# Transposed sums through ScalarE and GpSimd, and the second quad's stacks three rounds later, in a sliding-window attention kernel

## The chip, the cores and the metric

The kernel runs on one core of a Trainium2 chip. The metric is the device time of one launch in microseconds; the time of a kernel is the median of several runs. A profile is one further execution, recorded by the hardware profiler; its time in the trace is the span.

## What is computed

Four residual layers over a sequence of 2048 tokens with 576 features: attention, spectral filter, attention, spectral filter. The weights are the same both times.

```python
S, D, H, Dh, W = 2048, 576, 32, 18, 256

def A(x, wqkv, wo):                      # sliding-window attention
    q, k, v = split_heads(x @ wqkv)      # 32 heads of 18
    s = q @ k.T * Dh ** -0.5
    s = where((i - j >= 0) & (i - j < W), s, -1e9)
    return merge_heads(softmax(s) @ v) @ wo

def B(x, w_r, w_i):                      # global filter
    return irfft2(rfft2(x) * (w_r + 1j * w_i))

for _ in range(2):
    x = x + A(layernorm(x), wqkv, wo)
    x = x + B(layernorm(x), w_r, w_i)
```

All is in float32. The output is x.

## The kernel before

**Stages.** The program is straight-line code made by Python loops, one stage for each layer: attention, filter, attention, filter. The change lies in the attention stages alone (`layer_a`, called for layer 0 and again for layer 1). In the profiled execution the bursts described below begin at about 132 us in layer 0 and at about 884 us in layer 1; the mixed part, with projections among the attention work, ends at about 420 and 1175 us, and the output projection follows.

**Precision.** Operands of the projections and scores are split in a high and a low part, so that several products are summed to one result. A projection of 128 rows for 512 tokens (`proj`) is 14 matmuls of 128x128 by 128x512 into one PSUM buffer; each of these matmuls is one *projection step* (line L798). When the 14 are done, ScalarE copies the high part to `sg` (L810), Vector makes the low part (L813), and a DMA puts both into `qk_d` in device memory (L815). Eight projections come ahead of everything else; 28 more, 392 steps, are in the list `pj` and are dealt out among the attention work, 70 of them in `opening`, 322 in `bursts`.

**Quads, blocks and rounds.** The 32 heads are eight quads of four. A quad has 16 blocks of 128 tokens. A *round* x is one block of one quad: x = 16 n + i for block i of quad n, 128 rounds in all. The four heads of a round lie as two pairs in two halves of the partitions.

- `score_max` (L855, L857): a matmul gives the scores of a block against the window's three blocks in a PSUM buffer of tag "S"; Vector adds the mask and keeps the maximum of each row.
- `m_rows(n, c)` (L868 to L875): the maxima of four blocks are transposed, ScalarE makes `mt` of them, and four small DMAs put them as extra rows into the stack of q, so that the next matmul subtracts them.
- `exps` (L892, L893, L895, L898): the scores are computed again transposed, with the maximum subtracted, into a buffer of tag "E"; ScalarE takes the exponent; once a round GpSimd sets what lies outside the window to zero by two masks over all four heads.
- `part` (L912, L917): products of the exponents with the values, with a column of ones behind the values, are summed in the bank `U`: 18 sums and the denominator for each head and token. Every fourth block ScalarE copies the bank to `us`.
- `norm(n, c)` (L926 to L936): four transposes turn `us` so that tokens lie on partitions, into a PSUM buffer that `turned` picks; Vector takes the reciprocal of the denominators (L929) and multiplies the sums by it (L931) straight from PSUM; a DMA (L936) puts the result into `o_d`.

The buffer of `turned` is of tag "E" in the opening, of tag "S" (the three buffers that the scores use in turn) while projections are left, and of tag "pj" afterwards. There are 31 norms in a layer; the last group of blocks of the last quad is done by other code at the stage's end, which the change leaves as it is.

**Stacks.** The scores read q and k from the stacks `qs` and `ks`, two of each, used by even and odd quads. `stack_load(n, c)` fills 512 tokens of one quad's stacks from `qk_d` by twelve DMAs of 72 KB each (L830), all on the SP queue. SP takes its instructions in program order; the rows of `m_rows` (for n > 0 or c > 1), the outputs of `norm`, the `qk_d` writes and the loads of values and weights are on the same queue. `loads(t)` says at which round a stack is called: for the second quad at rounds t = 0, 4, 8 and 12, for later quads at t = 16 n - 20 + 4 c.

**Order.** The scores run `LEAD` = 10 rounds ahead of the exponents: round x of the exponents stands beside round x + 10 of the scores. The second quad's scores begin at round 6. `bursts` writes the order out by hand. Burst k holds three score matmuls and three exponent matmuls, since a round has four of each. Three bursts in every eight or so then hold products with the values (`values`); the others hold projection steps. The steps are cut into 23 units, each 14 steps over the bursts up to `ends[i]`, dealt out as evenly as it goes (`steps`), two to five in a burst. A burst with projection steps may also take a task from `due`, maxima rows first and then norms: two projection steps are written ahead of the task, the rest behind it.

**Names in the profile.** `tpo` is the transposed tile of a norm, `rc` the reciprocal, `o` its result, `tpm` the transposed maxima, `qs<-qk_d` and `ks<-qk_d` a stack's loads, `qs<-mt` the rows of maxima, `ofree<-o_d` the load of the attention's result for the output projection.

The call of the stacks before:

```python
c, r = divmod(t + (16 if n == 1 else 20) - NT * n, 4)
if r == 0 and 0 <= c < 4:
    stack_load(n, c)
```

Of the kernel before, what the change touches and what calls it, by code (L numbers as in the profile page):

```python
# [8 lines left out]
F32 = mybir.dt.float32  # L9
# [9 lines left out]
NT = 16  # L19
# [589 lines left out]
def layer_a(tc, ident, eps, bp, src, dst, wqk_d, wv_d, wo_d, dc_d, gc_d, dram, copy, wvs, second, spectral, share):  # L609

    nc = tc.nc
    V, A, T, P = nc.vector, nc.scalar, nc.tensor, nc.gpsimd
# [14 lines left out]
    if True:  # L627
# [134 lines left out]
        with ExitStack() as c2:  # L762
            wp = c2.enter_context(tc.tile_pool(name="a2", bufs=2))
# [8 lines left out]
            for j in range(2):  # L772
                q = wp.tile([128, 2, S], F32R, name=f"qs{j}", bufs=1)
                k = wp.tile([128, 2, S], F32R, name=f"ks{j}", bufs=1)
# [85 lines left out]
            def turned(name):  # L860

                tag = "E" if done < 70 else "S" if done < len(pj) else "pj"
                return pp.tile([128, 4, 128], F32, tag=tag, name=name, bufs=1 if tag == "pj" else 3)
# [59 lines left out]
            def norm(n, c):  # L923
                tp = turned(f"tpo{n}_{c}")
                for a in range(4):
                    T.transpose(tp[:, a], us[n, c][:, a * 128:a * 128 + 128], ident)  # L926
                tv = tp.rearrange("p a (h e) -> p (a h) e", e=32)
                rc = wp.tile([128, 16, 1], F32, tag="rc", name=f"rc{n}_{c}", bufs=2)
                V.reciprocal(rc, tv[:, :, 18:19])  # L929
                o = wp.tile([128, 4, 72], F32, tag="o", name=f"o{n}_{c}", bufs=2)  # L930
                V.tensor_mul(o.rearrange("p a (h e) -> p (a h) e", e=18), tv[:, :, 0:18], rc.to_broadcast([128, 16, 18]))  # L931
                lo, hi = 72 * n, 72 * n + 72
                for a, f0, f1 in ((o_d, 0, 448), (o7_d, 448, 576)):
                    b, e = max(lo, f0), min(hi, f1)
                    if b < e:
                        nc.sync.dma_start(a[c * 512:(c + 1) * 512, b - f0:e - f0].rearrange("(a p) e -> p a e", a=4), o[:, :, b - lo:e - lo])  # L936
# [13 lines left out]
            pj = [f for i in range(2, 9) for c in range(4) for f in proj(i, c, c % 2 if i == 2 else c == 0 and i == 3)]  # L950
# [4 lines left out]
            def loads(t):  # L955
                if t + LEAD in (0, 2):
                    stack_load(0, 2 + (t + LEAD) // 2)
                for n in range(1, NQ):
                    c, r = divmod(t + (16 if n == 1 else 20) - NT * n, 4)
                    if r == 0 and 0 <= c < 4:  # L960
                        stack_load(n, c)
                if t + LEAD == 5:
                    v_load(0)
                if t + 12 in range(NT, NX, NT):
                    v_load((t + 12) // NT)
# [27 lines left out]
            def bursts():  # L993

                es = [(x, pair, hp) for x in range(MIX) for pair in range(2) for hp in range(2)]
                ss = [(x + LEAD, pair, 1 - hp) for x, pair, hp in es]
                parts = [(x, half) for x in range(MIX - 2) for half in range(2) if x % NT]
                values = {(4 * x + 7) // 3 + 2 for x in range(0, MIX - 2, 2)}
                ends = [3] + [max(k - 1 for k in values if k - 1 <= 4 + 134 * (i + 1) // 22) for i in range(22)]
                steps = {}  # L1000
                for i, end in enumerate(ends):
                    ks = [k for k in range(ends[i - 1] + 1 if i else 0, end + 1) if k not in values]
                    steps.update({k: 14 // len(ks) + (z < 14 % len(ks)) for z, k in enumerate(ks)})
                at = 70
                for k in range(-(-len(es) // 3)):
                    e, c = es[3 * k:3 * k + 3], ss[3 * k:3 * k + 3]
                    for x, pair, hp in e:
                        if pair == hp == 0:
                            loads(x)
                            assert not any(source(p) == x - 6 for p in parts)  # L1010
                    score_max(*c[0])
                    for f in e:
                        exps(*f)
                    for f in c[:0:-1]:
                        score_max(*f)
                    remainders()

                    new, took = [], 0
                    spread = at == len(pj)
                    while parts and (took < 430 or source(parts[0]) < e[0][0] - 3 if spread else took == 0 or parts[0][0] % 2 or parts[0][1]):  # L1020
                        if (4 * source(parts[0] if spread else (parts[0][0] | 1, 1)) + 3) // 3 + 2 > k:
                            break
                        x, half = parts[0]
                        if took and half == 0 and (x % 4 == 0 or x % NT == 1):
                            break
                        parts.pop(0)
                        part(x, half)
                        took += lasting((x, half))
                        if half and x % 4 == 3:
                            new.append((norm, *divmod(x // 4, 4)))  # L1030

                    due.sort(key=lambda z: z[0] is norm)
                    tasks = [] if took and not spread else due[:1 + (len(due) > 2)]
                    del due[:len(tasks)]
                    n = steps.get(k, 0)
                    for f in pj[at:at + min(2, n)]:
                        yield f
                    for f, *a in tasks:
                        f(*a)
                    for f in pj[at + 2:at + n]:  # L1040
                        yield f
                    at += n

                    full = (3 * k + len(e)) // 4 + LEAD - 1
                    if (3 * k) // 4 + LEAD - 1 < full and full % 4 == 3:
                        new.append((m_rows, *divmod(full // 4, 4)))
                    due.extend(new)
                    for x, pair, hp in e:
                        if pair == hp == 1:
                            behind(x)  # L1050
                remainders()
                assert at == len(pj)
                for p in parts:
                    part(*p)
                    if p[1] and p[0] % 4 == 3:
                        due.append((norm, *divmod(p[0] // 4, 4)))
# [59 lines left out]
            for k in range(4):  # L1116
                tp = pp.tile([128, 512], F32, tag="E" if k else "pj", name=f"tpz{k}", bufs=3 if k else 1)[0:32]
                for a in range(4):
                    T.transpose(tp[:, 128 * a:128 * a + 128], us[NQ - 1, 3][:, 4 * k + a:512:16], ident)
                tv = tp.rearrange("p (a h e) -> p a h e", a=4, h=4)  # L1120
                rc = wp.tile([128, 4, 4, 1], F32, tag="rc", name=f"rcz{k}", bufs=2)[0:32]
# [5 lines left out]
            tp = pp.tile([128, 512], F32, tag="pj", name="tpl", bufs=1)  # L1127
# [58 lines left out]
```

## Time and profile before

| | us |
|---|---|
| median of 3 runs | 1508.76 |
| lowest and highest | 1503.93, 1511.95 |
| profiled execution, device time | 1516.93 |
| its span in the trace | 1515.2 |

The profiled execution is 8.17 us above the median of the other three, and 1.73 us of its time lie outside its span. Its mean granted TensorE clock is 0.989 of full speed. In rows of the profile PE is TensorE's matmul, PEld its weight load, DVE is Vector, ACT is ScalarE, POOL is GpSimd, SP (SPq) the queue that issues most DMAs. A row of the timeline gives start and duration in us, engine, line, operation, tiles and shapes, how many alike, and in brackets the idle time before and what ended it by the profile. A row of groups gives the count, then busy us and the mean in ns, then idle time before. A row of windows gives the stretch and its length, then busy time and count of each engine, the granted clock, the DMA engines' busy share and GB/s.

### The profile page before, as it was taken

The numbers are of one execution on the slowest core, as the hardware profiler recorded it, in microseconds if no ns is written. First come the engines' busy times: TensorE is split into PE (matmuls) and PEld (weight loads), VectorE is DVE, ScalarE is ACT, GpSimd is POOL, SyncE is SP. The second block draws the span as 40 slices with busy tenths as digits, with TensorE's granted clock in tenths as the row PEclk, the third lists the DMA queues.
The fourth block names the chain that finished last, engine by engine and source line by source line (L and its number), as shares of the span: only waits on it lengthen the run. The fifth ranks groups of instructions, "written<-read, shape, count | busy, mean of one in ns | idle before, by whom it ended". The sixth has DMA issues, their size and how long they took to land.

```text
span 1515.2 us, 34681 instructions
## 1 busy us (share of the span) xinstructions
PE 1447.9 (96%) x12124; PEld 1105.0 (73%) x12124; DVE 968.8 (64%) x3152; ACT 790.0 (52%) x1900; POOL 623.0 (41%) x1026
## 2 busy tenths in 40 slices
PE   7999999999999899999999999999999998999998
PEld 7975566666656799759999756666666568997598
DVE  5328787878883555447852377878788835554476
ACT  5524667666675443224454246667666754442243
POOL 2173345445454333243421833444444543322434
PEclk9999999999999999999999999999999999999999
DMA  6755556655545365767663556565554454657664
GB/s 194 199 168 182 182 179 195 181 177 168 157 134 160 120 217 184 240 204 236 240 168 92 179 185 176 170 166 152 153 153 131 129 160 137 212 187 237 211 209 141
DMA packets 203132, 267.64 MB, mean 177 GB/s; under 512 B 103183, under 2 KB 108303, under 8 KB 201999
## 3 DMA queue, kind: packets, MB, share of 16 engines
q1 hardware_dynamic: 194510, 245.41, 53.4%
q10 hardware_dynamic: 7808, 15.62, 3.1%
q0 software_dynamic: 640, 4.39, 1.0%
q8 instruction: 97, 1.59, 0.5%
q14 instruction: 77, 0.62, 0.1%
HBM read 166.71 MB, written 102.00 MB: 177 GB/s over the span
## 4 chain that ended last, share of the span: by engine, by line
PE 70%; DMA 10%; DVE 6%; ACT 4%; POOL 2%; issue 2%; SPq 1%; ACTq 0%; POOLq 0%; DVEq 0%
PE pj L798 15%; PE S L855 11%; PE U L912 10%; PE ops L555 6%; PE E L892 5%; PE vps L738 4%; PE pf L202 3%; PE pz L215 3%; DMA qs<-mt 3%; DMA ofree<-yd 2%; PE pq L313 2%; PE p L294 2%; PE pi L361 2%; PE tpo L926 2%; PE po L382 2%
## 5 line engine op out<-in xcount | busy, mean ns | idle before, releaser
L857 DVE CUSTOM_DVE_ANT_0 jk<-S,mask 128x384 bf16<-128x384 f32 (+2 forms) x1024 | 491.5, 529 | 129.2 <-PE E L892 71.4
L893 ACT ACTIVATE P<-E 128x384 f32<-128x384 f32 (+2 forms) x1024 | 409.5, 476 | 172.2 <-PE E L892 137.2
L895 POOL TENSOR_SCALAR_AFFINE_SELECT P<-P 128x512 f32<-128x512 f32 x256 | 162.4, 634 | 370.2 <-ACT P L893 347.9
L855 PE MATMUL S<-ks,qs 63*128 63x384 f32 (+2 forms) x1024 | 281.6, 373 | 4.2 <-DMA qk_d<-sg 2.4
L892 PE MATMUL E<-qs,ks 64*128 64x384 f32 (+2 forms) x1024 | 223.7, 373 | 7.9 <-DMA qs<-mt 4.5
L855 PEld LDWEIGHTS S<-ks,qs 63*128 63x128 f32 x1024 | 145.1, 185 | 114.7 <-DVE m L857 69.0
L912 PE MATMUL U<-P,vq 128*19 128x128 f32 (+1 forms) x3840 | 188.4, 329 | 1.0 <-ACT us L917 1.0
L798 PE MATMUL pj<-xh,wqh 128*128 128x512 f32 x360 | 156.9, 436 | 2.8 <-ACT vt L742 1.7
L912 PEld LDWEIGHTS U<-P,vq 128*19 128x19 f32 x3840 | 96.0, 98 | 78.9 <-issue 21.2
L898 POOL TENSOR_SCALAR_AFFINE_SELECT P<-P 128x512 f32<-128x512 f32 x224 | 142.0, 634 | 0.0
L892 PEld LDWEIGHTS E<-qs,ks 64*128 64x128 f32 x1024 | 112.8, 185 | 23.9 <-ACT P L893 14.2
L555 PE MATMUL ops<-oroom 128*128 128x288 f32 x840 | 123.8, 304 | 4.4 <-DVE oroom L538 3.0
L798 PE MATMUL pj<-xh,wql 128*128 128x512 f32 x360 | 125.8, 421 | 0.4 <-POOL wql L460 0.4
L798 PE MATMUL pj<-xl,wqh 128*128 128x512 f32 x288 | 120.7, 419 | 0.0
L555 PEld LDWEIGHTS ops<-oroom 128*128 128x128 f32 x840 | 115.9, 193 | 6.2 <-DVE oroom L538 4.0
L798 PEld LDWEIGHTS pj<-xh,wqh 128*128 128x128 f32 x360 | 67.7, 188 | 34.7 <-issue 11.3
L171 POOL TENSOR_TENSOR eo<-xn 128x287 f32<-128x287 f32 x32 | 26.1, 816 | 153.4 <-ACT xn L169 142.3
L813 DVE TENSOR_TENSOR sg<-pj,sg 128x512 fp32r<-128x512 f32 x72 | 49.5, 687 | 58.2 <-ACT sg L810 58.1
L857 DVE DVE_READ_ACCUMULATOR2_ANT m<- 128x1 f32 x1024 | 84.9, 83 | 0.0
L361 PE MATMUL pi<-oroom 128*128 128x256 f32 (+1 forms) x576 | 77.6, 289 | 5.8 <-ACT oroom L346 5.1
L798 PEld LDWEIGHTS pj<-xh,wql 128*128 128x128 f32 x360 | 64.6, 190 | 23.0 <-issue 11.2
L361 PEld LDWEIGHTS pi<-oroom 128*128 128x128 f32 (+1 forms) x576 | 73.1, 187 | 7.6 <-ACT oroom L346 5.8
(177 smaller groups left out, 2575.2 us busy)
## 6 DMA issues: line engine op xcount, KB each, us to landing
qk_d<-sg SPq DMA_DIRECT2D x56, 512.0 KB
qs<-qk_d SPq DMA_DIRECT2D x384, 72.0 KB
ks<-qk_d SPq DMA_DIRECT2D x384, 72.0 KB
v_d<-vt SPq DMA_DIRECT2D x32, 304.0 KB
vq<-v_d SPq DMA_DIRECT2D x16, 608.0 KB
yd<-ye SPq DMA_DIRECT2D x32, 290.0 KB
wt<-in_w SPq DMA_DIRECT2D x16, 580.0 KB
x<-ofree SPq DMA_DIRECT2D x32, 288.0 KB
```

Source lines behind the costliest of these rows:

```text
L361: T.matmul(o, z[:, sl, c, lo:lo + m], mo, start=k == 0, stop=k == 5)
L555: self.nc.tensor.matmul(self.ps[u][n][:, 0:288], x, self.w[p][:, wk * D + n * 288:wk * D + n * 288 + 288], start=first and i == 0, stop=la ...
L738: T.matmul(ps[:, n, 0:288], xT(xk, c), w[:, wk, n * 288:(n + 1) * 288], start=i == 0, stop=i == len(ks) - 1)
L798: T.matmul(box["ps"].rearrange("r (n p) -> r n p", n=NT) if second else box["ps"], w[:, wk], x, start=s == 0, stop=s == len(ks) - 1)
L813: V.tensor_sub(rest[:, 1], by, rest[:, 0].bitcast(F32))
L855: T.matmul(ps[:, 0:N], q[b:b + 63, pair, i * 128:i * 128 + 128], k[b:b + 63, pair, lo:hi], start=True, stop=True)
L857: V.tensor_tensor_reduce(out=jk[:, 0:N], in0=ps[:, 0:N], in1=mask[:, 384 - N:384], scale=1.0, scalar=-3e38, op0=ALU.add, op1=ALU.max, accu ...
L892: T.matmul(ps[:, 0:nq], k[b:b + 64, pair, j * 128:j * 128 + 128], q[b:b + 64, pair, j * 128:j * 128 + nq], start=True, stop=True)
L893: A.activation(p[:, hl_, 0:nq], ps[:, 0:nq], AF.Exp, scale=SC)
L895: P.affine_select(out=p[:, :, 0:128], in_=p[:, :, 0:128], pattern=[[0, 4], [1, 128]], compare_op=ALU.is_ge, fill=0.0, base=0, channel_mult ...
L898: P.affine_select(out=p[:, :, 256:384], in_=p[:, :, 256:384], pattern=[[0, 4], [-1, 128]], compare_op=ALU.is_gt, fill=0.0, base=0, channel ...
L912: T.matmul(U[32 * h:32 * h + 19, (q0 % 4) * 128:(q0 % 4) * 128 + 128 * (q1 - q0)], vts[n][:, j, h], pt[n, j][:, h, (q0 - j) * 128:(q1 - j) ...
```

## The change

In `norm` the four transposes are followed by a ScalarE copy of 19 of each 32 columns from PSUM into a new tile `ts` in SBUF (one buffer). The reciprocal reads `ts` instead of PSUM and stays on Vector. The multiply reads `ts` and runs on GpSimd (`P`) instead of Vector. The last group's code at the stage's end still uses Vector.

In `loads` the second quad's stacks are called at t = 3, 7, 11 and 15, three rounds later each. Their first calls thereby move from bursts 0, 5, 10 and 16 to bursts 4, 9, 14 and 20. The calls for other quads stay. Stack (2,0) is called at t = 12, which was the round of stack (1,3) and is now ahead of it.

In `bursts` the units and their ends stay, but the steps of a burst are worked out as it is written: what is left of the unit over the bursts left in it, rounded up, and one more (at most five, and leaving two for each burst that follows) where the burst holds a norm and is not its unit's last. Later bursts of the unit get fewer. The total is the same. In bursts with fewer than four steps one step, not two, is written ahead of the task.

```diff
@@ norm
-                tv = tp.rearrange("p a (h e) -> p (a h) e", e=32)
+                ts = wp.tile([128, 16, 19], F32, tag="ts", name=f"ts{n}_{c}", bufs=1)
+                A.copy(ts, tp.rearrange("p a (h e) -> p (a h) e", e=32)[:, :, 0:19])
                 rc = wp.tile([128, 16, 1], F32, tag="rc", name=f"rc{n}_{c}", bufs=2)
-                V.reciprocal(rc, tv[:, :, 18:19])
+                V.reciprocal(rc, ts[:, :, 18:19])
                 o = wp.tile([128, 4, 72], F32, tag="o", name=f"o{n}_{c}", bufs=2)
-                V.tensor_mul(o.rearrange("p a (h e) -> p (a h) e", e=18), tv[:, :, 0:18], rc.to_broadcast([128, 16, 18]))
+                P.tensor_mul(o.rearrange("p a (h e) -> p (a h) e", e=18), ts[:, :, 0:18], rc.to_broadcast([128, 16, 18]))
@@ loads
-                    c, r = divmod(t + (16 if n == 1 else 20) - NT * n, 4)
+                    c, r = divmod(t + (13 if n == 1 else 20) - NT * n, 4)
@@ bursts
-                steps = {}
-                for i, end in enumerate(ends):
-                    ks = [k for k in range(ends[i - 1] + 1 if i else 0, end + 1) if k not in values]
-                    steps.update({k: 14 // len(ks) + (z < 14 % len(ks)) for z, k in enumerate(ks)})
+                unit = {k: i for i, end in enumerate(ends) for k in range(ends[i - 1] + 1 if i else 0, end + 1)}
...
-                    n = steps.get(k, 0)
-                    for f in pj[at:at + min(2, n)]:
+                    n = 0
+                    if k in unit and k not in values:
+                        gaps = sum(z not in values for z in range(k, ends[unit[k]] + 1))
+                        rest = 70 + 14 * (unit[k] + 1) - at
+                        n = -(-rest // gaps)
+                        if gaps > 1 and any(f is norm for f, *a in tasks):
+                            n = min(5, n + 1, rest - 2 * (gaps - 1))
+                    early = 1 if n < 4 else 2
+                    for f in pj[at:at + min(early, n)]:
                         yield f
                     for f, *a in tasks:
                         f(*a)
-                    for f in pj[at + 2:at + n]:
+                    for f in pj[at + early:at + n]:
                         yield f
```

## The prediction

> **What bounds the kernel now.** I read the page first: the span, the busy shares and the split of the chain that ended last.
>
> ```profile
> span 1515.2 us, 34681 instructions
> PE 1447.9 (96%) x12124; PEld 1105.0 (73%) x12124; DVE 968.8 (64%) x3152; ACT 790.0 (52%) x1900; POOL 623.0 (41%) x1026
> PE 70%; DMA 10%; DVE 6%; ACT 4%; POOL 2%; issue 2%; SPq 1%; ACTq 0%; POOLq 0%; DVEq 0%
> ```
>
> TensorE is busy for 96% of the span and is 70% of the chain, so an edit that leaves its work alone gains only where TensorE waits, and loses only where it makes TensorE wait. Next come the windows (busy time and count of PE, PEld, DVE, ACT, POOL, then clock, DMA share, GB/s) of layer 0's attention: all engines from 189.38 to 420, then the score matmuls L855 alone.
>
> ```profile
> 189.38:420.00 230.62, 229.92 (x2289) 143.96 (x2288) 185.75 (x732) 158.55 (x400) 110.45 (x178) 1.00 0.59 175
> 189.38:420.00 230.62, 93.14 (x337) 48.05 (x337) 1.00 0.59 175
> ```
>
> 337 score matmuls at three to a burst are 112 bursts, 230.62 / 112 = 2.06 us each. Vector is busy for 81% of this stretch, GpSimd for 48%, ScalarE for 69%. "PE busy" counts a matmul that is waiting in the pipeline too, so the stalls have to be read from the weight loads. Here are the loads of two neighbouring bursts; the first holds a norm (norm is the step that the change rewrites), the second feels it.
>
> ```profile
> 258.07 0.18 PEld L855 LDWEIGHTS S<-ks,qs 63*128 63x128 f32 x1 [0.21 <-DVE m L857]
> 258.36 0.19 PEld L855 LDWEIGHTS S<-ks,qs 63*128 63x128 f32 x2
> 258.80 0.19 PEld L798 LDWEIGHTS pj<-xh,wqh 128*128 128x128 f32 x1 [0.26 <-DVE sg L813]
> ...
> 260.14 0.18 PEld L855 LDWEIGHTS S<-ks,qs 63*128 63x128 f32 x1 [0.25 <-DVE m L857]
> 260.43 0.19 PEld L855 LDWEIGHTS S<-ks,qs 63*128 63x128 f32 x1
> 260.88 0.18 PEld L855 LDWEIGHTS S<-ks,qs 63*128 63x128 f32 x1 [0.26 <-PE E L892]
> 261.25 0.19 PEld L798 LDWEIGHTS pj<-xl,wqh 128*128 128x128 f32 x1 [0.19 <-issue]
> 261.36 0.19 PEld L798 LDWEIGHTS pj<-xh,wqh 128*128 128x128 f32 x1
> 261.59 0.19 PEld L798 LDWEIGHTS pj<-xl,wqh 128*128 128x128 f32 x1
> ```
>
> After 258.07 the first projection load comes 0.73 us behind the first score load; after 260.14 it comes 1.11 behind, because the third score load stands back until 260.88. That is 0.38 us lost. The row names a score matmul, but Vector and ScalarE show what was late:
>
> ```profile
> 260.01 0.26 DVE L929 RECIPROCAL rc<-tpo 128x16 f32<-128x16 f32 x1
> 260.31 0.46 DVE L931 TENSOR_TENSOR o<-tpo,rc 128x288 f32<-128x288 f32 x1
> 258.58 1.25 ACT L893 ACTIVATE P<-E 128x384 f32<-128x384 f32 x3 [0.81 <-PE E L892]
> 260.65 0.49 ACT L893 ACTIVATE P<-E 128x384 f32<-128x384 f32 x1 [0.81 <-PE E L892]
> ```
>
> The transposed sums sit in one of the three "S" buffers, and Vector gives it back at 260.77, just ahead of the load at 260.88. So the norm costs TensorE time through a buffer, not through its own work.
>
> The other place where TensorE waits is the start of each layer's bursts, which I call the ramp. The SP queue there, then the loads that had idle time before them (150 to 187: layer 0; 902 and 916: layer 1):
>
> ```profile
> 144.69 2.86 SPq L830 DMA_DIRECT2D ks<-qk_d  x6
> 158.33 2.46 SPq L875 DMA_DIRECT2D qs<-mt  x4
> 161.33 3.02 SPq L830 DMA_DIRECT2D qs<-qk_d  x6
> 164.39 3.03 SPq L830 DMA_DIRECT2D ks<-qk_d  x6
> 176.18 2.67 SPq L830 DMA_DIRECT2D qs<-qk_d  x6
> 178.89 2.82 SPq L830 DMA_DIRECT2D ks<-qk_d  x6
> 182.87 3.27 SPq L875 DMA_DIRECT2D qs<-mt  x4
> 186.24 2.23 SPq L830 DMA_DIRECT2D qs<-qk_d  x6
> ```
>
> ```profile
> 150.64 0.18 PEld L855 LDWEIGHTS S<-ks,qs 63*128 63x128 f32 x1 [1.10 <-issue]
> 151.33 0.18 PEld L892 LDWEIGHTS E<-qs,ks 64*128 64x128 f32 x1 [0.51 <-issue]
> 163.21 0.18 PEld L892 LDWEIGHTS E<-qs,ks 64*128 64x128 f32 x1 [1.26 <-ACT P L893]
> 186.85 0.18 PEld L892 LDWEIGHTS E<-qs,ks 64*128 64x128 f32 x1 [0.64 <-ACT us L917]
> 902.69 0.18 PEld L855 LDWEIGHTS S<-ks,qs 63*128 63x128 f32 x1 [1.80 <-issue]
> 916.82 0.18 PEld L892 LDWEIGHTS E<-qs,ks 64*128 64x128 f32 x1 [1.42 <-ACT P L893]
> ```
>
> Each such wait ends 2 to 3 us after SP has issued the transfers in question: the last piece of stack (1,0) is issued by 147.55 and the score matmul that needs it loads at 150.64, 3.1 us later; the four rows of maxima are issued by 160.79 and the exponent matmul loads at 163.21. The waits are 1.10 + 0.51 + 1.26 + 0.64 = 3.51 us in layer 0 and 1.80 + 1.42 = 3.22 in layer 1, 6.7 together.
>
> **The norm.** Both layers have 31 norms through this code. The edit adds a ScalarE copy of 128x304, turns the reciprocal to SBUF, and moves the multiply from Vector to GpSimd. The nearest rows (busy us, mean ns): a ScalarE copy out of PSUM, two GpSimd arithmetic operations of nearly this width, and GpSimd's masks.
>
> ```profile
> L742 ACT COPY vt<-vps 128x288 f32<-128x288 f32 x64 | 22.4, 402 | 41.7 <-issue 21.0 <-PE vps L738 18.5 <-ACT wqh L459 2.2
> L302 POOL TENSOR_TENSOR uv<-ofree 128x290 f32<-128x290 f32 x32 | 22.3, 698 | 76.9 <-DVE ofree L298 76.9
> L393 POOL TENSOR_TENSOR xo<-xo,bs 128x287 f32<-128x287 f32 x32 | 35.6, 1114 | 0.0
> L895 POOL TENSOR_SCALAR_AFFINE_SELECT P<-P 128x512 f32<-128x512 f32 x256 | 162.4, 634 | 370.2 <-ACT P L893 347.9 <-DMA qk_d<-sg 11.6 <-ACT mt L870 9.5
> ```
>
> ScalarE is free from 258.58 + 1.25 = 259.83 until 260.65, and the reciprocal's start shows the transposes done by 260.01. A copy of 0.41 fits and returns the buffer at 260.42, 0.35 ahead of before. The change also puts one more projection step into the norm's burst (0.23 us, the distance of the loads at 261.36 and 261.59), so the third score matmul comes later by that as well. 0.35 + 0.23 is more than 0.38: the stall goes. The total of projection steps is unchanged, so the redistribution itself costs nothing; a shorter later burst is covered as long as its Vector work keeps up, and would otherwise cost up to 0.2 per norm, the lower end below.
>
> Of the 24 norms of a layer that lie beside projections, three fall in the ramp, seven stand in bursts that already have five steps and lose nothing, nine in bursts of three (0.38 each) and four or five in bursts of four (a step more covers 0.23 of it: 0.15). That is 9 x 0.38 + 4 x 0.15 = 4.0 per layer, **-8.0** for two; -3 if a third of it comes back through late copies or thin bursts, -9 at most.
>
> The multiply takes 0.70 to 1.11 on GpSimd instead of 0.46 on Vector (I take 0.9), and starts a copy later, so `o` is ready 0.6 to 1.1 us later. In the mixed stretch only its DMA waits, and what SP has queued behind it. GpSimd's two masks of a round queue behind the multiply, which waits for ScalarE and the reciprocal; the values that read them come at least two bursts, 4.1 us, later, and GpSimd is idle for 52% of the stretch: nothing.
>
> **The second quad's stacks.** Twelve DMAs each; four stacks move from bursts 0, 5, 10 and 16 to 4, 9, 14 and 20, while their scores stay at 8, 13, 18 and 24. The lead becomes four bursts, 4 x 2.06 = 8.2 us. A stack takes SP 4.5 us (twice 2.23) to 6.05 (3.02 + 3.03), I take 5.2, and 3.1 to land: 8.3. So it is late by 0.1 plus whatever SP still has in hand at the call. For (1,0) and (1,1) that is the four rows of maxima called one burst earlier: 2.5 long, sent only when the maxima are done, so 1.0 to 2.3 is left; 1.6, late by 1.7 each. For (1,2) it is the output of norm (0,1), which now waits for GpSimd: 0.3 to 1.0, late by about 0.9. For (1,3) the order of calls turns round: stack (2,0) and the rows (1,1) are now ahead of it. From burst 14 SP has 0.5 of output, 5.2 of (1,2), 2.5 of rows (1,0), 5.2 of (2,0) and 2.9 of rows (1,1): 16.3 in six bursts, 12.4. Of the 3.9 left, 0.9 passes while TensorE waits for (1,2): 3.0, late by 3.1. The sum is 7.4 per layer.
>
> In return the rows of maxima are called ahead of the stacks instead of behind them, and all the old waits go. Net: 2 x 7.4 - 6.7 = **+8.1**. At 4.5 per stack and the low remainders the four are late by 0.4, 0.4, 0 and 1.3: 4.2 - 6.7 = -2.5. At 6.05 they are late by some 11 per layer, since each wait gives SP time: +15.
>
> A wait has a second cost. Some 2 us after the waits that ended at 902.69 and 916.82 the granted clock is halved:
>
> ```profile
> 905.00:908.00 3.00, 3.00 (x21) 0.50 0.64 176
> 918.60:921.60 3.00, 3.00 (x14) 0.50 0.57 159
> ```
>
> That is 1.5 us lost in each stretch. I expect about two again, behind the waits for (1,3), so nothing net; six of them, behind all waits of over 1.4, would be +6. The Trainium skill, "TensorE: Matmul & The Clock Gate", Part 1, has the clock fall after at least one idle window of about 3.4 us. By that rule no wait of 1.80 or 1.42 could have done it, nor would the new ones of 3.1 do it, and this term has no upper end; the rows speak for a shorter wait.
>
> **The tail.** Behind the last projections the output's DMA lies on the chain:
>
> ```profile
> 476.26 6.37 DMA o_d<-o
> ```
>
> Its norm is later by 0.41 + 0.9 - 0.46 = 0.85 per layer: **+1.7**; zero if another wait is as late, +3.5 if ScalarE, which is dense there with exponents, delays the copy as well.
>
> **Sum.** -8.0 + 8.1 + 1.7 = +1.8. The profiled execution took 1516.93 (8.2 over the median 1508.76 of the runs shown), so 1518.7 by its clock, and **1510.6** against the median. Half a per cent, 7.5 us, is about what a measurement of this kernel can tell from no change.
>
> **Rivals.**
> - *The stacks are in time.* With SP at 2.23 for six and the early rows out of the way, every wait of the ramp goes: -8.0 - 6.7 + 1.7 = -13.0, 1495.8. For it: 186.24, the pace once the queue is short, and that the old waits were half for rows, which now go first. Against it: (1,0) was late with eight bursts of lead.
> - *SP does not keep up.* At the pace of 161.33, four stacks late by 11 per layer: +15; the norm gains 6 and the tail costs 3: +12, 1520.8. Its place is burst 24; it decides once stack (1,3) lands more than 4 us after the first score of that burst is due. For it: SP issues without a break from 161.33 to 167.42 and from 176.18 to 181.71.
> - *The reciprocal waits for GpSimd.* It now reads and writes SBUF while GpSimd masks SBUF for 48% of the time. One Vector operation of that kind ran beside GpSimd arithmetic with a spread of ten (ns, min/median/max):
>
> ```profile
> L349 DVE CAST oroom<-oroom x32: 196/571/2211, 682.8 to 1502.5; 128x66 fp32r<-128x66 f32 x32
> ```
>
> If the reciprocal waits half a mask of 0.634 in 48% of cases, 0.15 each, 48 norms cost 7.4 of a Vector that is 81% full: +9.2 in all, 1518.0. The Trainium skill, "SBUF — State Buffer", section "SBUF: two separate sides", calls the port pair that Vector and GpSimd share an exclusive lock, held for a whole instruction. The row of L349 agrees; that a reciprocal takes the lock no run here shows.
>
> That the change does not do what it says (the stall moves to another "S" user) would leave -3 in place of -8: 1515.6, inside the main case's range.
>
> **Chances.** The sum above 0.50, with its own range of 1504 to 1517 (0.43 within half a per cent, 0.07 slower); stacks in time 0.22 (0.19 faster, 0.03 the same); SP behind 0.18 (slower); the reciprocal 0.10 (0.08 slower, 0.02 the same). That makes faster 0.19, same 0.48, slower 0.33. The range 1496 to 1521 cuts the two outer rivals in half, 0.2 in all.
>
> **What would show it.** Right: in norm bursts the third score load comes about 0.45 us after the first, with no gap, and the projections of the burst behind start 0.73 after its first score load, not 1.11; score loads of the second quad wait 1 to 3 us at four places of each ramp, behind SP's stack rows, the last one longest; no exponent matmul there waits for rows of maxima; the new multiply averages 0.7 to 1.1 on GpSimd. Wrong: a ramp as long as before or shorter, a reciprocal above 0.35, or masks so late that the values wait for GpSimd.

## The result and the profile after

| | before | changed |
|---|---|---|
| median (6 runs each), us | 1509.76 | 1523.97 |
| lowest and highest | 1503.93, 1511.98 | 1518.49, 1524.61 |
| ratio to before, 95% interval | | 1.0089 [1.0066, 1.0113] |
| profiled execution, its span | 1516.93, 1515.2 | 1521.42, 1519.4 |

The change makes the kernel slower by 10 to 17 us, 13.4 by the ratio. Measured again later, beside other kernels, it was 1.0056 [1.0038, 1.0073], 8.5 us. The forecast was 1510.6 with a range from 1496 to 1521.

From the page of the changed kernel, busy time and chain:

```profile
PE 1440.4 (95%) x12124; PEld 1097.5 (72%) x12124; DVE 943.2 (62%) x3090; ACT 812.2 (53%) x1962; POOL 665.5 (44%) x1088
PE 68%; DMA 9%; DVE 6%; ACT 5%; POOL 2%; SPq 2%; issue 2%; ACTq 0%; POOLq 0%; DVEq 0%
```

62 instructions more on ScalarE and on GpSimd and 62 fewer on Vector are the norm's move; TensorE has as many as before and a smaller share. The windows by stage, columns as before: the ramp (first score matmul of burst 0 to that of burst 25), then the mixed stretch (to burst 132), of layer 0 and of layer 1; first the kernel before, then the changed one.

```profile
131.78:189.38 57.60, 53.63 (x470) 32.60 (x470) 42.27 (x164) 36.69 (x90) 22.33 (x35) 1.00 0.65 203
189.38:409.87 220.49, 219.80 (x2194) 137.75 (x2194) 178.18 (x700) 151.24 (x382) 105.56 (x170) 1.00 0.60 179
883.71:943.81 60.10, 55.75 (x470) 33.87 (x470) 42.35 (x164) 36.86 (x90) 22.28 (x35) 0.94 0.67 197
943.81:1164.98 221.17, 220.37 (x2195) 137.60 (x2195) 178.15 (x700) 151.26 (x382) 97.82 (x154) 1.00 0.56 158
```

```profile
133.03:199.23 66.20, 54.72 (x469) 33.33 (x469) 41.15 (x161) 37.82 (x93) 24.36 (x38) 0.90 0.58 188
199.23:416.78 217.55, 217.17 (x2195) 135.80 (x2195) 169.96 (x679) 158.92 (x402) 120.24 (x191) 1.00 0.59 177
885.86:952.49 66.63, 56.85 (x470) 34.38 (x469) 41.14 (x161) 37.86 (x93) 24.35 (x38) 0.89 0.60 185
952.49:1171.08 218.59, 218.04 (x2194) 135.45 (x2194) 169.92 (x679) 158.92 (x402) 111.99 (x175) 1.00 0.55 156
```

The two ramps take 132.8 us in place of 117.7, the two mixed stretches 436.1 in place of 441.7. So both halves of the change show, with opposite signs, and the loss is larger. Ramps (+15.1), mixed stretches (-5.6) and the layers' ends (+2.0, below) sum to +11.5, between the two measured losses. In the ramps the DMA share falls, from 0.65 and 0.67 to 0.58 and 0.60, and the clock from 1.00 and 0.94 to 0.90 and 0.89. Share times length says that the DMA engines are busy for 37 and 40 us of the two ramps before and for 38 and 40 after: they do the same work in a longer time, while TensorE stands.

**The norm's place.** The burst behind the norm that was shown ahead of the change, now at 269.46 (weight loads, then the norm itself on Vector, ScalarE, GpSimd):

```profile
269.46 0.18 PEld L855 LDWEIGHTS S<-ks,qs 63*128 63x128 f32 x1 [0.36 <-DVE m L857]
...
269.74 0.19 PEld L855 LDWEIGHTS S<-ks,qs 63*128 63x128 f32 x2
270.18 0.19 PEld L798 LDWEIGHTS pj<-xh,wqh 128*128 128x128 f32 x1 [0.25 <-issue]
```

```profile
269.61 0.25 DVE L930 RECIPROCAL rc<-ts 128x16 f32<-128x16 f32 x1 [0.45 <-ACT ts L928]
269.10 0.41 ACT L928 COPY ts<-tpo 128x304 f32<-128x304 f32 x1 [0.17 <-PE tpo L926]
269.95 0.68 POOL L932 TENSOR_TENSOR o<-ts,rc 128x288 f32<-128x288 f32 x1
```

The first projection comes 0.72 us after the burst's first score load, not 1.11: the stall is gone. Vector, however, now stands 0.45 us ahead of its reciprocal, until ScalarE's copy is done; what it saves by the multiply (0.46) it loses by waiting. Over all 62 norms its idle time ahead of the reciprocal is 57.6 us, where it was 29.8.

**The ramp.** TensorE's waits in the changed kernel (150 to 196: layer 0; 907 to 949: layer 1), at bursts 8, 13, 18 and 24, and SP's queue in layer 0:

```profile
153.58 0.28 PEld L855 LDWEIGHTS S<-ks,qs 63*128 63x128 f32 x1 [3.53 <-issue]
167.16 0.18 PEld L855 LDWEIGHTS S<-ks,qs 63*128 63x128 f32 x1 [0.58 <-DVE m L857]
178.47 0.22 PEld L855 LDWEIGHTS S<-ks,qs 63*128 63x128 f32 x2 [1.60 <-DVE m L857]
195.30 0.28 PEld L855 LDWEIGHTS S<-ks,qs 63*128 63x128 f32 x1 [5.51 <-issue]
907.06 0.28 PEld L855 LDWEIGHTS S<-ks,qs 63*128 63x128 f32 x1 [4.03 <-issue]
921.05 0.18 PEld L855 LDWEIGHTS S<-ks,qs 63*128 63x128 f32 x1 [0.55 <-issue]
932.65 0.21 PEld L855 LDWEIGHTS S<-ks,qs 63*128 63x128 f32 x2 [1.90 <-issue]
948.56 0.28 PEld L855 LDWEIGHTS S<-ks,qs 63*128 63x128 f32 x1 [3.17 <-issue]
```

```profile
142.10 2.76 SPq L875 DMA_DIRECT2D qs<-mt  x4
144.91 3.72 SPq L830 DMA_DIRECT2D qs<-qk_d  x6
148.67 2.15 SPq L830 DMA_DIRECT2D ks<-qk_d  x6
...
156.41 2.47 SPq L875 DMA_DIRECT2D qs<-mt  x4
158.93 2.35 SPq L830 DMA_DIRECT2D qs<-qk_d  x6
161.32 2.97 SPq L830 DMA_DIRECT2D ks<-qk_d  x6
...
164.87 5.54 SPq L937 DMA_DIRECT2D o_d<-o  x2
170.46 2.24 SPq L830 DMA_DIRECT2D qs<-qk_d  x6
172.75 2.15 SPq L830 DMA_DIRECT2D ks<-qk_d  x6
175.32 2.48 SPq L875 DMA_DIRECT2D qs<-mt  x4
177.90 2.51 SPq L830 DMA_DIRECT2D qs<-qk_d  x6
180.46 2.66 SPq L830 DMA_DIRECT2D ks<-qk_d  x6
183.21 0.39 SPq L815 DMA_DIRECT2D qk_d<-sg  x1
183.70 0.41 SPq L937 DMA_DIRECT2D o_d<-o  x1
184.19 3.00 SPq L875 DMA_DIRECT2D qs<-mt  x4
187.24 2.29 SPq L830 DMA_DIRECT2D qs<-qk_d  x6
189.56 2.15 SPq L830 DMA_DIRECT2D ks<-qk_d  x6
```

All these waits are now of score matmuls (L855), none of an exponent matmul for rows of maxima. They sum to 11.2 us in layer 0 and 9.7 in layer 1, 20.9, where there were 6.7. Stack (1,3) is the last pair of rows: SP ends it at 191.71, burst 24 starts on it at 195.30. In a second profile of the same kernel the waits at bursts 8 and 24 were 3.67 and 5.86 in layer 0, 5.05 and 3.16 in layer 1, so a single wait can move by a microsecond from one execution to the next. SP is not busy all the time: it stands for the rows of maxima ahead of 156.41, and within the row of 164.87, whose two outputs are issued 5.2 us apart.

### The profile page after: what moved, and what is told of

It is laid out like the page before. It is cut to its first block, busy times and chain, and to the rows that moved or that the text cites. A ratio compares the mean times of both kernels' runs of the same rounds, so it can differ in the third digit from the quotient of the medians.

```text
span 1519.4 us, 34771 instructions
## 1 busy us (share of the span) xinstructions
PE 1440.4 (95%) x12124; PEld 1097.5 (72%) x12124; DVE 943.2 (62%) x3090; ACT 812.2 (53%) x1962; POOL 665.5 (44%) x1088
## 4 chain that ended last, share of the span: by engine, by line
PE 68%; DMA 9%; DVE 6%; ACT 5%; POOL 2%; SPq 2%; issue 2%; ACTq 0%; POOLq 0%; DVEq 0%
PE pj L798 15%; PE S L855 11%; PE U L912 9%; PE ops L555 6%; PE E L892 4%; PE vps L738 4%; PE pf L202 3%; PE pz L215 3%; PE pq L313 2%; PE tpo L926 2%; PE pi L361 2%; PE p L294 2%; ACT P L893 2%; PE po L382 2%; DMA ofree<-yd 2%
## 5 line engine op out<-in xcount | busy, mean ns | idle before, releaser
L855 PE MATMUL S<-ks,qs 63*128 63x384 f32 (+2 forms) x1024 | 272.3, 375 | 19.7 <-DMA ks<-qk_d 8.5
L855 PEld LDWEIGHTS S<-ks,qs 63*128 63x128 f32 x1024 | 142.6, 188 | 126.7 <-DVE m L857 74.7
L555 PE MATMUL ops<-oroom 128*128 128x288 f32 x840 | 120.8, 299 | 4.4 <-DVE oroom L538 3.0
L555 PEld LDWEIGHTS ops<-oroom 128*128 128x128 f32 x840 | 112.8, 189 | 6.2 <-DVE oroom L538 4.0
L798 PEld LDWEIGHTS pj<-xh,wql 128*128 128x128 f32 x360 | 64.9, 191 | 21.1 <-issue 11.2
```

The source lines that it names most:

```text
L555: self.nc.tensor.matmul(self.ps[u][n][:, 0:288], x, self.w[p][:, wk * D + n * 288:wk * D + n * 288 + 288], start=first and i == 0, stop=la ...
L798: T.matmul(box["ps"].rearrange("r (n p) -> r n p", n=NT) if second else box["ps"], w[:, wk], x, start=s == 0, stop=s == len(ks) - 1)
L855: T.matmul(ps[:, 0:N], q[b:b + 63, pair, i * 128:i * 128 + 128], k[b:b + 63, pair, lo:hi], start=True, stop=True)
```

## The experiments

All ratios are to the kernel before, run on the same chip; not all the kernels ran on one chip. Ramps and mixed stretches are sums over both layers, bounded like the windows above, in one profiled execution each; in brackets the half-clock windows (3.41 us each) that begin in the two together.

| kernel | ratio [95%] | ramps | mixed |
|---|---|---|---|
| before (two profiles) | | 117.7, 117.8 | 441.7, 441.4 (2, 2) |
| changed (two profiles) | 1.0089, 1.0056 | 132.8, 132.3 | 436.1, 434.9 (9, 7) |
| new norm, stacks as before | 0.999 [0.9971, 1.0009] | 117.7 | 436.3 (3) |
| stacks only | 1.0109 [1.0081, 1.0138] | 133.0 | 442.4 (6) |
| next quads later | 1.0045 [1.0025, 1.0065] | 128.4 | 436.0 (5) |
| multiply on Vector | 1.003 [1.001, 1.005] | 116.8 | 443.3 (2) |
| tail as before | 0.9944 [0.9921, 0.9967] | 119.7 | 435.4 (4) |
| even steps | 0.9975 [0.9957, 0.9992] | 116.0 | 435.5 (2) |
| steps only | 0.997 [0.995, 0.999] | 117.8 | 438.2 (3) |
| waits filled, more filled | 1.0034, 1.0023 | 131.1, 129.2 | 435.3, 436.2 (2, 0) |
| two rounds | 1.0003 [0.9979, 1.0028] | 121.8 | 435.4 (6) |
| one round earlier | 0.9965 [0.9948, 0.9982] | 122.5 | 434.8 (5) |
| one stack later | 0.9982 [0.9963, 1.0] | 120.8 | 434.9 (3) |

### The change in halves

The changed kernel with `13` put back to `16`:

> The changed kernel with one number put back: the second quad's stacks are called where they were before (t = 0, 4, 8, 12). The norm on ScalarE and GpSimd and the dealt-out steps stay. Theory (the stacks make it slower, the norm part is a gain): 24 norm places a layer give back about 0.3 to 0.4 us at each burst with three or four steps, 3.5 us a layer behind the ramp by the two traces, 1 more in the ramp; so 8 us under the kernel before, about 1502. Rival A (GpSimd's slower multiply and the later outputs on the SP queue cost as much as the buffer gives): within 3 us of the kernel before, about 1510. Rival B (the new deal of the steps makes the ramp slower): 1515 or more.

The kernel before with `16` turned to `13`:

> The kernel before with one number changed: the second quad's stacks called three rounds later. Theory (stacks alone): the ramps get longer by 14 to 17 us together, 16.4 in the trace of the changed kernel with its norm gains there already taken off, so about 1510 + 16 = 1526. Rival (the outputs that wait for GpSimd ahead of stack (1,2) on the SP queue carry the lateness on to (1,3)): the third and fourth waits shrink to under 1 and 3 us, about 1518.

The stacks alone cost 1.09%, 16.5 us, as the theory had it. The rival holds for the third wait alone: at burst 18 it was 0.95, where the changed kernel has 1.60, so the outputs that wait for GpSimd cost 0.6 us there. The wait at burst 24 was as long without them (kernel with the stacks alone, weight loads, then SP's outputs ahead of stack (1,2)):

```profile
176.98 0.21 PEld L855 LDWEIGHTS S<-ks,qs 63*128 63x128 f32 x2 [0.95 <-DVE m L857]
194.29 0.28 PEld L855 LDWEIGHTS S<-ks,qs 63*128 63x128 f32 x1 [5.88 <-issue]
```

```profile
162.77 5.84 SPq L936 DMA_DIRECT2D o_d<-o  x2
```

With the multiply on Vector SP stands in that row as long (5.84 us, in the changed kernel 5.54): what it waits for is mostly norm (0,1) itself, on whichever engine that is done.

The norm half came to -1.5 us [-4.4, +1.4], not the -8 expected. Its mixed stretches are shorter by 5.4, so something was given back elsewhere: its ramps gained nothing (117.7), and the layers' ends lose, as shown below.

### Which part of the norm works, and where it costs

```diff
-  P.tensor_mul(o..., ts[:, :, 0:18], rc...)     # multiply on Vector
+  V.tensor_mul(o..., ts[:, :, 0:18], rc...)
```

> The changed kernel with the stacks called where they were before, and the norm's multiply back on Vector, reading the copy in SBUF. The windows to read are the mixed stretch (bursts 25 to 132 of each layer), 220.4 and 221.2 us before and 218.4 and 217.9 with the norm on ScalarE and GpSimd, and the tail (from the last burst to the first matmul of the next layer's filter), 120.4 us for both layers less the half-clock windows before and 123.1 with the new norm. Theory (the buffer's early return by ScalarE carries the gain, GpSimd is not needed for it): the mixed stretch stays within 0.5 us of 218, the tail falls by 0.5 to 1 of its 2.7. Rival (Vector's share carries the gain, it is 81% busy there): the mixed stretch goes back to over 220.

The theory fell. The mixed stretches went to 443.3, longer than before the change (441.7). ScalarE's copy gives the buffer back, but Vector waits for that copy with the maxima queued behind it; unless the multiply leaves Vector, the wait only costs. The groups of that kernel, with Vector's idle time ahead of the reciprocal, beside that of the kernel before:

```profile
L930 DVE RECIPROCAL rc<-ts 128x16 f32<-128x16 f32 x62 | 15.7, 254 | 55.1 <-ACT ts L928 55.1
L932 DVE TENSOR_TENSOR o<-ts,rc 128x288 f32<-128x288 f32 x62 | 30.5, 492 | 2.1
```

```profile
L929 DVE RECIPROCAL rc<-tpo 128x16 f32<-128x16 f32 x62 | 15.9, 257 | 29.8 <-PE tpo L926 29.4
```

Idle ahead of it rose from 29.8 to 55.1 us over 62 norms, 0.41 each, which is the copy's length.

The projection steps dealt evenly, with the new norm, and the new deal with the old norm:

> The changed kernel with the stacks called where they were before and the projection steps dealt out evenly, as before the change: the norm on ScalarE and GpSimd alone. Theory (the buffer comes back 0.35 us earlier, which is nearly the stall of 0.38): the mixed stretch is 218 to 219 us in each layer. Rival (the step more in a norm's burst hides the stall): it stays above 220.

> The kernel before with the new deal of the projection steps alone; norm and stacks as before. Theory (the buffer): one step of 0.23 hides part of the 0.38 in nine bursts a layer, so the mixed stretch gains about 2 us and is near 219; tail and ramp as before. Rival (the deal alone carries the whole gain): the mixed stretch is at 218 or less.

The new norm alone shortens the mixed stretches by 6.2 us, the new deal alone by 3.5, both together, over all the kernels that have both, by 5.4 to 6.9: the deal adds little or nothing on top of the norm. Its bursts of two projection steps are a likely reason, not tested by themselves: in the changed kernel burst 62 has two steps and lasts 1.58, and the burst of values behind it 2.27 in place of 2.09.

The norms behind the last projection done as before:

```diff
+  mixed = done < len(pj)
+  if mixed:
       ts = wp.tile(...); A.copy(ts, tv[:, :, 0:19]); tv = ts
   V.reciprocal(rc, tv[:, :, 18:19])
-  P.tensor_mul(o..., ts[:, :, 0:18], rc...)
+  (P if mixed else V).tensor_mul(o..., tv[:, :, 0:18], rc...)
```

> The changed kernel with the stacks called where they were before, and with the norms behind the last projection done as before (reciprocal and multiply on Vector, straight from PSUM). Theory (copy and GpSimd multiply lie on the chain at each layer's end): the tail goes back from 123.1 to 120.4 us for both layers, half-clock windows taken off, the mixed stretch stays at 218; 2.7 under the kernel with the norm everywhere and about 4 under the kernel before. Rival (the tail is longer because of another wait, such as the transfers in flight): the tail stays at 122 or more and the time is that of the kernel before within 2 us.

This is the best version measured: 0.9944, 8.5 us under the kernel before [5, 12]. Call the tail of a layer the time from the first score matmul of its last burst (157) to the first matmul of the filter (L185). In profiles that have no half-clock window there the two tails sum to 94.8, 94.6 and 94.4 us with the new norm in them (changed kernel, the two with filled waits) and to 92.4 and 92.8 with the old (steps only, one round earlier): 2.0 us. With the copy kept and the multiply on Vector they were 94.1 in the one profile, so most of it seems to go with the copy. The chain of the changed kernel shows where both lie:

```profile
481.14 0.42 ACT ts L928
481.93 0.68 POOL o L932
482.60 0.19 POOL ofree L464
482.85 0.42 SPq L520
483.37 5.78 DMA o_d<-o
```

Copy and multiply are links of the chain, and GpSimd's L464, for which SP's L520 waits ahead of the output, is queued behind the multiply. The rest of the 7 us between this version (0.9944) and the one with the norm everywhere (0.999) is not explained; they ran on different chips. Its own profile accounts for about 4 us against the kernel before: 6.3 won in the mixed stretches, 2.0 lost in the ramps, which held two more half-clock windows. As the lowest of many ratios, and with 0.9965 and 0.9982 for the two kernels built on it below, 0.9944 may flatter it.

### Why the stacks are late

```diff
-  c, r = divmod(t + (13 if n == 1 else 20) - NT * n, 4)
+  c, r = divmod(t + (13 if n == 1 else 16) - NT * n, 4)
```

> The changed kernel with the stacks of quads 2 to 7 called four rounds later too (at 16 n - 16 + 4 c in place of 16 n - 20 + 4 c), so that stack (1,3) is called ahead of (2,0), as before the change. Theory (the turned order makes the fourth wait): the wait at burst 24, 5.51 us in layer 0 and 3.17 in layer 1, falls to about 1 in both and its half-clock windows go: 7 to 9 us under the changed kernel, about 1516. Rival (a stack needs more than four bursts whatever is ahead of it): the fourth wait stays at 2 to 3 us, like that at burst 8: 1520 or more.

The waits at burst 24 fell to these, from 5.51 and 3.17:

```profile
193.72 0.28 PEld L855 LDWEIGHTS S<-ks,qs 63*128 63x128 f32 x1 [3.49 <-issue]
945.58 0.18 PEld L855 LDWEIGHTS S<-ks,qs 63*128 63x128 f32 x1 [2.69 <-issue]
```

So the turned order is worth about 2.0 us in layer 0. The 0.5 of layer 1 can't be told from chance: the wait at burst 8, which comes ahead of all that this edit moves, went from 3.53 to 4.46 in layer 0. Most of the wait stays, as the rival said, whose cause is the lead itself. Two rounds later instead of three (`14`):

> The changed kernel with the second quad's stacks called two rounds later than before the change instead of three (t = 2, 6, 10, 14), which makes their calls bursts 2, 8, 13 and 18, leads of 6, 5, 5 and 6 bursts in place of 4, and puts three of the four ahead of the rows of maxima again. Theory (the lead is too short for what SP has in hand): the score waits at bursts 8 and 24 fall by the two bursts, 4.1 us, to 0 and 1.4 at most, those at 13 and 18 go; rows of maxima cost about 1 us again at two places; the time is that of the kernel with the stacks where they were, within 4 us, about the time of the kernel before. Rival (stack (2,0) called ahead of (1,3) and the outputs from GpSimd hold the queue whatever the lead): the wait at burst 24 stays over 2 us and the time is 6 us or more above the kernel before.

1.0003: the loss goes with the shorter lead, although stack (2,0) is still called ahead of (1,3) here. Three of the four stacks are also ahead of the rows of maxima again, so lead and order are not wholly separated. In layer 0 burst 8 still waits 3.04 us and burst 24 1.48, and an exponent matmul waits for rows again, at 911.87 for 1.44. The other way, from the best version, one round earlier (`17`), and only stack (1,1) later (t = 0, 7, 8, 12):

> The best version so far (norm on ScalarE and GpSimd beside projections, as before at the layer's end, new deal of steps) with the second quad's stacks called one round earlier than before the change (t = -1, 3, 7, 11), so that each is right behind a call of rows of maxima, as in the change, with nine bursts of lead. Theory (order and lead both count): the waits for rows at bursts 13 and 24, 1.2 to 1.4 and 0.6 to 1.3 us in the layers, fall by half or more; 2 to 4 us under that version, 1501 to 1503. Rival (SP is backed up from the opening until burst 8, so the calls change nothing there): the same waits, the same time within 1 us.

> The version with the new norm beside projections, the norm as before at the layer's end and the new deal of steps, and of the second quad's stacks only (1,1) called three rounds later (t = 7), behind the rows of maxima (0,3); the others stay at t = 0, 8 and 12. Theory (which of the four moves helps depends on what is ahead on SP at that place): the wait for the rows at burst 13, 1.91 and 2.27 us in that version, goes, and the score matmul waits 0.5 to 0.7 there, as in the changed kernel; the waits at 18 stay at zero; 2 to 4 us under that version's ratio to the kernel before of 0.9944, so about 0.992. Rival (the four-burst lead is too short at every place): the score wait at burst 13 is 1.5 or more and the ramp is as long as in that version or longer.

Neither helped. With the stacks earlier the exponent matmuls at burst 13 wait longer for their rows (first row below; 3.53 in layer 1, where the best version had 1.91 and 2.27); with one stack later its scores wait (second row):

```profile
166.71 0.28 PEld L892 LDWEIGHTS E<-qs,ks 64*128 64x128 f32 x1 [2.96 <-issue]
913.91 0.28 PEld L855 LDWEIGHTS S<-ks,qs 63*128 63x128 f32 x1 [3.05 <-issue]
```

SP has the same transfers to issue in every order: what it puts first is early, and what it puts second waits. That is a reading of these runs, not the whole of it: with the stacks earlier the rows left SP at 162.71 and the matmul came 4.0 us later, in the best version 2.65 us later, and why they took longer is not shown.

### The clock

The kernel before once more:

> The kernel before, profiled once more. If the profiled execution shown with it was long because of half-clock windows outside the attention (seven of them, against three in the profile of the changed kernel), this one has another number of such windows, its time differs by about 1.7 us for each, and its bursts agree within 0.1 us each except next to such windows. Otherwise its windows lie at the same places and its time is within 1 us of 1516.9.

It took 1510.9 us, 6.0 less than the first profiled execution, with six half-clock windows where that had nine (the program's last microseconds aside): two in layer 0's ramp, where the first had none, and none in layer 1's, where the first had two. Of the 214 bursts of the mixed stretches all but one agreed to 0.03 us. So the windows are not at fixed places, and a single execution's time carries them. They also give a price: layer 0's ramp took 59.6 us with its two windows and 57.6 without any, at nearly the same waits, about a microsecond for each; layer 1's took 58.2 without and 60.1 with two.

```diff
+  if k in (8, 24):                      # in the other run {8: 16, 13: 4, 18: 4, 24: 16}
+      dm = pp.tile([128, 512], F32, tag="S", name=f"dm{k}", bufs=3)
+      for z in range(12):
+          T.matmul(dm, xT(0, slice(0, 128)), xT(0, slice(0, 512)), start=True, stop=True)
   score_max(*c[0])
```

> The changed kernel with twelve more matmuls of 128x128 by 128x512 into an unread score buffer at the head of bursts 8 and 24 of each layer, where TensorE waits for a stack 3.2 to 5.5 us; at 0.23 each they are 2.8 us and lie inside the waits. They are no part of the computation. Theory (the waits cost a second time, through the granted clock): the half-clock stretches in the two ramps, nine windows of 3.41 us in the trace of the changed kernel, fall to three or fewer; a window is up to 1.7 us of lost work, by the bursts next to the waits 8.9 us in all, so the time falls by 4 to 8 us. Rival (the matmuls only prolong the chain, or half clock is hidden beside the waits): the same time or up to 3 us more, and the windows stay.

> The changed kernel once more, beside the next kernel on the same chip, since the loss and the filled waits were measured on different chips. Theory and rival alike: 0.6 to 1.1% above the kernel before; windows of half clock in the ramps between five and nine.

> The changed kernel with unread matmuls at the head of four bursts of each layer: 16 at bursts 8 and 24, 4 at 13 and 18, 0.23 us each, so 3.7 and 0.9 us, inside waits of 3.2 to 5.5 and 0.6 to 1.9. They are no part of the computation. Theory (waits cost a second time through the clock): at most two half-clock windows in both ramps, the time 5 to 9 us under the changed kernel on the same chip, at 0.2 to 0.5% above the kernel before, which is the waits' own length. Rival (the clock's share is small and the earlier gain was the chip's): within 3 us of the changed kernel, or above it.

With two waits filled, two half-clock windows were left and the ratio was 1.0034, on another chip than the changed kernel. TensorE's windows over both ramps (layer 0, layer 1; length, busy time and count of TensorE alone, clock, DMA share, GB/s), the changed kernel again and then, on the same chip, the one with all four waits filled:

```profile
133.00:205.00 72.00, 60.24 (x512) 0.91 0.57 184
885.00:960.00 75.00, 64.08 (x534) 0.93 0.57 176
```

```profile
133.00:205.00 72.00, 67.88 (x568) 1.00 0.57 184
885.00:960.00 75.00, 71.72 (x611) 1.00 0.61 187
```

With the waits covered by work that nobody needs the clock stays at 1.00, and the kernel goes from 1.0056 to 1.0023, 5.0 us. The two intervals, [1.0038, 1.0073] and [1.0003, 1.0043], overlap, and the ramps and mixed stretches of the two profiles differ by only 1.8 us (567.2 and 565.4); the unread matmuls may also have lengthened the chain in places. Seven windows more than before at about a microsecond each would be 7. So half clock has a part in the loss, by these readings 2 to 7 us; its size stays open.

## Why the prediction was wrong

**Forecast and result.** The sum was +1.8 us; measured were +13.4 and +8.5. Of the rivals, "SP does not keep up" (+12, chance 0.18) comes nearest in size. Its sign, stack (1,3) more than 4 us late, came in layer 0 (5.51) and not in layer 1 (3.17); its cause, a pace of 6.05 for each stack, came only at (1,0) in layer 0 (5.9).

**The step that failed is the ramp's term, +8.1.** In the profiles it is 132.8 - 117.7 = +15.1, and +15.3 with the stacks alone. That the rows' waits go and four score waits come was right. The sizes were not: the four waits sum to 20.9 us over both layers, not 14.8. One by one:
- (1,0), late by 1.7, was 3.53 and 4.03. SP still had 2.9 us in hand at the call (the rows run from 142.10 to 144.86, the burst began at 141.99), not 1.6, since the rows are sent only when ScalarE has made them; and the stack took SP 5.9 us, not 5.2.
- (1,1), 1.7, was 0.58 and 0.55. In layer 0 SP had 2.0 us in hand at the call and the stack took 5.4, both a little over the sum; but the four bursts of lead took 9.2 us in place of 8.2, at half clock until 159.24. A slower TensorE gives SP time, which the sum didn't have.
- (1,2), 0.9, was 1.60 and 1.90. SP stands in the outputs' row of 164.87 until GpSimd has multiplied norm (0,1), with the stack behind it, which starts 1.6 us after the burst of its call. With the multiply on Vector it started 1.1 after it, and the wait was 0.95 and 0.99: the sum's 0.9 is what comes without GpSimd, whose part of 0.6 to 0.9 came on top.
- (1,3), 3.1, was 5.51 and 3.17. It starts at 187.24, behind stack (2,0) and the rows (1,1), as forecast, and the stacks took SP no longer than the sum had it (4.4, 5.2 and 4.5 us). In layer 0 the rest came from links that it had too short or not at all: the late start of (1,2) (1.1 us more), a `qk_d` write and an output at 183.21 and 183.70 (0.9), and 3.6 us from the last issue to the matmul in place of 3.1. In layer 1, where stack (2,0) took 4.4 and the landing 3.1, the wait was close to the forecast.

**The clock's term was zero and had an end at +6.** Nine windows came where I expected two; the 2 to 7 us that they may be worth lie inside the ramp's +15.1. The waits of 3.17 us and more all had a window, but so had the one of 1.90 at 932.65 and, before the change, those of 1.42 and 1.80; in the second profiles one of 1.82 (kernel before) and one of 3.16 (changed kernel, burst 24 of layer 1) had none. At the wait that ended at 153.58 the clock fell at 152.41, 2.4 us after the wait began. The Trainium skill's "TensorE: Matmul & The Clock Gate", Part 1, lets the clock fall after an idle window of about 3.4 us. Here shorter waits were enough, though not each time; what share of idle time decides, these rows don't show.

**The norm's term, -8.0, was somewhat too large and partly wrong in cause.** The mixed stretches of the changed kernel gained 5.6 and, in its second profile, 6.8 us. By the trace ten norms of a layer, not nine, stand in bursts of three, so the sum as it was meant is -8.8. The buffer was the cause of the stall, but the added step is not what hides it (even steps: -6.2), and the early return alone is not enough either: with the multiply on Vector the stretch got longer. The prediction did not see that Vector waits for ScalarE's copy in front of its queue.

**The tail's term, +1.7, was 2.0.** The third rival is out: 62 reciprocals beside GpSimd lasted 252 to 256 ns.

## What to carry to other kernels

A queue that works in order has little free room even where it isn't always busy, since it also stands for inputs that aren't ready. Moving transfers behind others that were late mainly changes which consumer waits. So before giving lead away, add up the whole queue from the call to the last landing: every link, the small ones too, with its longest value beside its middle one. Not tried here: sending the norm's outputs on another queue, so that the stacks don't stand behind them. Moving an operation to another engine through a copy pays only if the engine that waits for the copy also loses work; and the same move can be right in one stage and wrong in another where it lies on the chain, so apply it by stage. Here waits of 1.4 us and more on TensorE were often, and those of over 3.2 always, followed or accompanied by half its clock for 3.4 to 10.2 us, where nothing filled them.

## What the hardware showed

- Half-clock stretches lasted 3.41 us or two or three times that, at places that changed from one execution of the same program to the next.
- GpSimd multiplied 128x288 by a broadcast column in 676 ns, against 457 on Vector from PSUM: 1.5 times, and with a spread of 664 to 692.
- Vector's multiply from SBUF lasted 457 to 918 ns beside GpSimd's masks, where its reciprocal from SBUF did not vary. Of the 62 multiplies 14 took more than 480 ns, each while a mask ran. The Trainium skill, "SBUF — State Buffer", section "SBUF: two separate sides", has a Vector operation with two inputs in SBUF wait for a GpSimd operation that reads SBUF, and these rows agree.
